# The beacon keys of sequences 2 to 7 loaded at the start and transposed early, with two projections moved

## The chip, the cores and the metric

The kernel runs on one core of a Trainium2 chip. The core has TensorE (PE in the profile; PEld is its weight load), VectorE (DVE), ScalarE (ACT), GpSimd (POOL) and SyncE (SP), and 16 DMA engines that move data between the device memory and the on-chip memories. SP, ACT and POOL can issue DMAs, each through a queue of its own (SPq, ACTq, POOLq in the profile). The metric is the device time of one execution in microseconds, lower is better.

## The reference

Attention with a few "beacon" keys in front, and then two matrix products with a leaky ReLU between them. Cut to what matters:

```python
# q, k, v: (8, 8, 576, 64); beacon_k, beacon_v: (8, 8, 16, 64)
k_all = np.concatenate([beacon_k, k], axis=2)         # 16 + 576 keys
v_all = np.concatenate([beacon_v, v], axis=2)
scores = np.matmul(q, k_all.transpose(0, 1, 3, 2)) / np.sqrt(64)
scores = np.where(causal, -1e9, scores)               # causal on the 576; beacon keys always seen
a = softmax(scores)
x = np.matmul(a, v_all)                               # -> (4608 tokens, 512)
h = x @ w_in                                          # w_in (512, 2048)
out = np.maximum(0.01 * h, h) @ w_out                 # w_out (2048, 512), out (4608, 512)
```

## The kernel before, in words

The work is cut into 32 pairs of heads: pair g is sequence g // 4 and two of its eight heads, whose 64 channels lie side by side in 128 partitions. For every pair the kernel needs queries and keys turned so that channels lie in partitions (qT, kT), the scores (keys in partitions, queries in columns), their exponentials in a buffer aT, the upper triangle set to zero on GpSimd (`triangle`, L281), and the values: aT against the values with a column of ones, so that the last column is the sum by which the rest is divided (`value`, L339; reciprocal L369 and product L370 on VectorE). The result is turned again into xT, either by transposes on PE (`x_transposes`) or by a DMA transpose on SP's queue (`x_turn`).

Behind that stand the two products, in nine chunks of 512 tokens. An up projection (`moe1`, L408: four matmuls of 128 x 512 at L413) makes 128 rows of the hidden layer, ScalarE applies the leaky ReLU (L420); 16 make a chunk. A down projection is a quarter of `moe2` (L446: four matmuls at L455); 16 make a chunk, and after every fourth VectorE copies the sum (L466) and SP stores it (L467). The first two down projections of a group of four read the first half of w_out, the other two the second half. In the code strings `u` is an up projection and `d` a down projection.

The beacon keys are 16 to a head. Those of all eight heads of a sequence fill 128 partitions; they are loaded (`load_beacon_k`, L176), cast to bf16 (`cast_beacon_k`, L179) and transposed on PE, two transposes to a sequence (`beacon_transposes`, L182). Sequences 0 and 1 are done at the very start and go straight into the first 16 columns of the key buffers. Sequences 2 to 7 go into bkT, from which GpSimd copies 16 columns per pair into a key buffer (`beacon_columns`, L219, step `b`), first for pairs 8 to 11.

The first eight pairs (sequences 0 and 1) follow an order written out by hand as strings of steps (L590 to L612), which `run` (L537) carries out. Each engine executes its own instructions in that order. The steps that matter here: `l` loads queries or keys of a pair with a cast, on POOL's queue; `q` and `k` turn them on PE (L235) with a copy on VectorE or ScalarE (L241); `s` is a quarter of a pair's scores with its exponential (L259, L268), `m` the triangles; `v` half of a pair's values; `V` a load of values (L206), `i` and `o` half of w_in and w_out (L123, L129), all on POOL's queue; `N` loads queries or keys of a later pair in their natural order (L163, POOL's queue) and `T` turns both of them by DMA transposes on SP's queue (L171); `y` is a turn of x by SP, `x` one by PE; `w` and `W` are matmuls of zeros whose result nobody reads (`unused`, L498, and `unused_ahead`, L510).

From pair 8 on the order is made by a list of events with due times (L638 to L677). The scores of pairs 8 to 31 are laid end to end and cut into tiles of 512 columns, three tiles to a `block` (L628); block m is due at 8.4 plus a step. Between events the loop puts in up and down projections by a linear plan (`fill`, L471).

The sums of PE live in two pools of PSUM: `ps_sc` for scores, and `ps_one`, four tiles shared by values, transposes, projections and the unused matmuls.

Of the kernel before, what the change touches and what calls it, by code (L numbers as in the profile page):

```python
# [8 lines left out]
FP32 = mybir.dt.float32  # L9
# [6 lines left out]
def kernel(  # L16
# [162 lines left out]
    def cast_beacon_k(b0, b1, copy):  # L179
        copy(out=bk[:, b0:b1], in_=bk_raw[:, b0:b1])  # L180
# [155 lines left out]

    xs, avs = {}, {}

    def value(g, half):  # L339
        b, hp = divmod(g, NPAIR)  # L340
        aT = probs[g]
        va = v_bufs[b % 2]
        if half == 0:
            xs[g] = (
                headpool.tile([128, 5, 2, D], BF16, name="x_nat", bufs=4),
                headpool.tile([128, 10], FP32, name="rec"),
            )
        x_nat, rec = xs[g]
        t0, t1 = ((0, 3), (3, 5))[half]
        av = avs.pop((g, half), None)  # L350
        if av is None:
            av = ps_one.tile([128, 512], FP32, name="av", tag="one")
        avv = av[:, 0 : (t1 - t0) * 132].rearrange("p (n w) -> p n w", w=66)
        for t in range(t0, t1):
            q0, _ = QT[t]
            for par in range(2):
                n = (t - t0) * 2 + par
                for c in range(t + 1):
                    a0 = acol(g, c, q0)
                    nc.tensor.matmul(  # L360
                        out=avv[:, n, 0 : D + 1],
                        lhsT=aT[0 : ROWS[c], par, a0 : a0 + 128],
                        rhs=va[0 : ROWS[c], c, 2 * hp + par, :],
                        start=(c == 0),
                        stop=(c == t),
                        skip_group_check=True,
                    )
        n0, n1 = t0 * 2, t1 * 2
        nc.vector.reciprocal(out=rec[:, n0:n1], in_=avv[:, :, D])  # L369
        nc.vector.tensor_tensor(  # L370
            out=x_nat[:, t0:t1].rearrange("p t e d -> p (t e) d"),
            in0=avv[:, :, 0:D],
            in1=rec[:, n0:n1, None].to_broadcast([128, n1 - n0, D]),
            op=ALU.mult,
        )
# [161 lines left out]
    def run(steps):  # L537
        for step in steps.split():
            op, a = step[0], [int(x) for x in step[1:].split(".")] if step[1:] else []
            if op == "s":  # L540
                score(*a)
            elif op == "m":
                mask(*a)
            elif op == "v":
                value(*a)
            elif op == "x":
                finish(*a)
            elif op == "l":
                load_qk(*a)
            elif op == "V":  # L550
                load_v_cast(*a)
            elif op == "N":
                load_natural(*a)
            elif op == "T":
                turn_pair(a[0])
            elif op == "y":
                x_turn(a[0])
            elif op == "q" or op == "k":
                t_q(a[0], 0 if op == "q" else 1, (dve, act)[a[1] if len(a) > 1 else 0])
            elif op == "b":  # L560
                beacon_columns(a[0], (dve, act, pool)[a[1]])
            elif op == "u":
                up()
            elif op == "P":
                moe1_early(*a)
            elif op == "d":
                down()
            elif op == "w":
                unused(*a)
            elif op == "W":  # L570
                unused_ahead(*a)
            elif op == "i":
                load_w_in(a[0])
            elif op == "o":
                load_w_out(a[0])
            else:
                raise ValueError(step)
# [11 lines left out]
    with order:  # L589
        load_first_keys()  # L590
        load_beacon_k(0, 2, nc.scalar)
        nc.vector.memset(blank, 0.0)  # L592
        run("l0.0 l1.0")
        make_identity(nc, ident)
        make_ones()
        run("l1.1 l2.0 l2.1 V0.0 V0.1 l3.0 l3.1 V0.2 V0.3 V0.4 l4.0 l4.1 i0")
        make_pads()
        unused(13, 256)
        cast_beacon_k(0, 2, nc.scalar.copy)
        beacon_transposes(0, 2)  # L600
        unused(13)
        nc.scalar.copy(out=k_nat0[:, :, 0], in_=first_k[:, 0])
        nc.vector.tensor_copy(out=k_nat0[:, :, 1], in_=first_k[:, 1])
        run("q0.1 k0 w2.384 s0.0 m0.0 w3.256 s0.1 q1 s0.2 m0.1 k1 s0.3 m0.2")
        run("w2.384 s1.0 m1.0 q2 s1.1 k2 w2.384 s1.2 m1.1 w2.384 s1.3 m1.2 W0.0.4 s2.0 m2.0 W0.0.4 s2.1 W0.0.2 q3 l5.0 l5.1 s2.2 k3 w3.384 v0.0 m2.1 s2.3 i1 m2.2 W0.1.4 s3.0 m3.0 v1.0 s3.1 v0.1 s3.2 v1.1 m3.1 l6.0 l6.1 s3.3 x0.1 m3.2")
        run("v2.0 V1.0 V1.1 q4 v2.1 x1 k4.1 v3.0 v3.1 x2.1 s4.0 s4.1 x3 m4.0 V1.2 V1.3 V1.4 l7.0 l7.1 u u s4.2 s4.3 q5 k5 m4.1 m4.2 u o0 u")
        load_beacon_k(2, B, nc.gpsimd)
        run("s5.0 s5.1 m5.0 u u u s5.2 s5.3 q6 k6 m5.1 m5.2 o1 u u s6.0 s6.1 m6.0 v4.0 u v4.1 y4 N8.0 N8.1 u u s6.2 s6.3 q7 k7 m6.1 m6.2 u")
        cast_beacon_k(2, B, nc.gpsimd.tensor_copy)
        run("u v5.0 u v5.1 N9.0 s7.0 s7.1 m7.0 d x5 v6.0 v6.1 T8 d s7.2 s7.3")  # L610
        beacon_transposes(2, B)
        run("m7.1 m7.2 N9.1 u b8.2 b9.2 b10.2 b11.2 x6 v7.0 T9 v7.1 d d N10.0 N10.1 d d V2.0 V2.1 x7 T10")  # L612


        FIRST = 2 * NPAIR
        COLS = FLAT[NKB]
        TILES = (NG - FIRST) * COLS // 512

        def tile_parts(n):
            at, end, parts = 512 * n, 512 * (n + 1), []  # L620
            while at < end:
                r, lo = divmod(at, COLS)
                hi = min(COLS, lo + end - at)
                parts.append((FIRST + r, lo, hi))
                at += hi - lo
            return parts

        def block(m):  # L628
            tiles = [tile_parts(n) for n in range(3 * m, min(3 * m + 3, TILES))]
            for n, parts in enumerate(tiles):  # L630
                stretch(parts, apart=n == 0)
            for parts in tiles:
                triangles(parts)

        def has_down():
            return done2[0] // NF < done1[0] // NF

        since = 0  # L638
        events = []
        for g in range(FIRST, NG):  # L640
            if g > FIRST + 2:
                events.append((g - 2.75, 0, run, ("N%d.0" % g,)))
                events.append((g - 2.45, 0, run, ("N%d.1" % g,)))
            if g > FIRST + 2:
                events.append((g - 1.75, 0, run, ("T%d" % g,)))
            if g > FIRST + 3:
                events.append((g - 1.65, 0, run, ("b%d.2" % g,)))
            at = g + (2.05 if g % NPAIR == NPAIR - 1 else 2.25)
            events.append((at, 3, value, (g, 0)))
            events.append((at + 0.37, 4, value, (g, 1)))  # L650
            events.append((at + 0.38, 5, x_turn, (g,)))
        for m in range((TILES + 2) // 3):
            events.append((FIRST + 0.4 + 1536 / COLS * m, 2, block, (m,)))
        ends = [FIRST]
        for g in range(FIRST, NG):
            events.append((g + 3.5, 2, finish, (g, 2)))
            if g % NPAIR == NPAIR - 1:
                ends.append(g + 3.5)
        for b in range(2, B):
            for n in range(2 if b == 2 else 0, NKB):  # L660
                events.append((4 * b + (-0.4 if b == 2 else -0.9) + 0.3 * n, 6, load_v_cast, (b, n)))
        events.sort(key=lambda e: e[:2])
        first_down[0] = 4
        w, d0 = 0, done1[0] + done2[0]
        for at, _, what, args in events:
            while w + 2 < len(ends) and at > ends[w + 1]:
                w, d0 = w + 1, done1[0] + done2[0]
            todo = 2 * NF * ready[0] - KEPT - d0
            aim = d0 + todo * (at - ends[w]) / (ends[w + 1] - ends[w])
            while done1[0] + done2[0] < aim and fill():  # L670
                pass
            if what is block:
                since = done1[0] + done2[0]
            elif what is value and not has_down():
                while done1[0] + done2[0] < since + 4 and fill():
                    pass
            what(*args)  # L677
        while done2[0] < NCH * NF:
            fill()
# [30 lines left out]
```

## Time and profile before

| | |
|---|---|
| median of five executions | 338.09 us |
| lowest and highest | 337.54 and 338.78 us |
| the profiled execution | 338.78 us |
| its span, first to last instruction | 337.1 us |
| PE matmul busy | 326.0 us |
| ScalarE busy | 187.1 us |
| GpSimd busy | 181.5 us |
| VectorE busy | 82.5 us |
| granted PE clock over the span | 1.000 |
| beacon keys of sequences 2 to 7: issue | 36.76 us, on POOL's queue |
| their cast on GpSimd | 47.67 us |
| their twelve transposes on PE | 50.32 us |
| first block of scores (pair 8) | 60.59 us |

A row of the timeline gives the start in us from the start of the span, the time from the first to the last of the merged instructions, engine, line, operation, what it writes and reads, how many, and in brackets the idle time of the engine just before it with what ended it. "issue" there means that the profile shows nothing it waited for. In the answer on DMA issues the last number is the time from the issue to the landing of the data. A row by stretches of time gives busy time of each engine in it, then the granted PE clock, the mean busy share of the DMA engines and GB/s. Matmul records are sometimes missing, so counts of 3 and 7 stand for 4 and 8.

### The profile page before, as it was taken

Reading aid. Unit: us, or ns where it says so; the run is one execution under the profiler, and the core shown is the slowest. Engines: PE = TensorE matmul, PEld = TensorE weight load, DVE = VectorE, ACT = ScalarE, POOL = GpSimd, SP = SyncE. Lnnn points to the kernel's source line nnn. Section 1 sums busy time; section 2 is a strip of 40 time slices with the busy share of each in tenths; the row PEclk is TensorE's granted clock in tenths of the full one; section 3 lists DMA queues with packets and bytes.
Section 4 is the critical chain, followed back from the end, with each engine's and each line's share of the span. In section 5 each row is a group of like instructions: output and inputs, shape, how many; then the busy total and the mean of one; then the engine's idle time right before and its main releaser. Section 6 shows DMA issues by size and latency. Waiting matters only on the chain.

```text
span 337.1 us, 7448 instructions
## 1 busy us (share of the span) xinstructions
PE 326.0 (97%) x2945; PEld 170.0 (50%) x2992; DVE 82.5 (24%) x201; ACT 187.1 (56%) x312; POOL 181.5 (54%) x355
## 2 busy tenths in 40 slices
PE   8999999899999999999999999999999999999996
PEld 5574465355554554554555555555455544444444
DVE  3472354021322113311321123212221310000111
ACT  5869762687565783488337843784378205633300
POOL 8895968878987785668656966674221000000000
PEclk9999999999999999999999999999999999999999
DMA  8999999999999999999999999999320120000012
GB/s 137 133 201 176 145 205 132 171 145 152 171 159 168 163 151 142 140 120 119 111 165 136 128 98 156 171 122 117 102 61 14 46 87 33 0 31 33 31 72 83
DMA packets 151922, 39.84 MB, mean 118 GB/s; under 512 B 143008, under 2 KB 145184, under 8 KB 151888
## 3 DMA queue, kind: packets, MB, share of 16 engines
q0 software_dynamic: 99824, 18.54, 85.9%
q1 hardware_dynamic: 51648, 20.64, 35.6%
q8 instruction: 23, 0.38, 0.5%
q10 hardware_dynamic: 416, 0.20, 0.2%
q14 instruction: 11, 0.09, 0.1%
HBM read 37.22 MB, written 9.44 MB: 138 GB/s over the span
## 4 chain that ended last, share of the span: by engine, by line
PE 82%; DMA 11%; POOL 3%; issue 2%; ACT 1%; DVE 0%; POOLq 0%; ACTq 0%; DVEq 0%
PE acc L455 35%; PE acc L413 33%; PE av L360 8%; PE sc L306 6%; DMA v_aug<-in_v_dram 5%; DMA w_in_sb<-in_moe_w_in_dram 4%; DMA k_nat<-in_k_dram 1%; DMA out_dram<-osb 1%; POOL v_aug L206 1%; POOL q_raw L151 0%; POOL aT L281 0%; PE sc L259 0%; POOL k_raw L151 0%; ACT aT L325 0%; POOL k_nat L163 0%
## 5 line engine op out<-in xcount | busy, mean ns | idle before, releaser
L413 PE MATMUL acc<-xT,w_in_sb 128*128 128x512 bf16 x553 | 134.4, 379 | 1.9 <-DVE osb L466 0.7
L455 PE MATMUL acc<-w_out_sb,gT 128*128 128x512 bf16 (+1 forms) x568 | 131.6, 373 | 1.5 <-issue 0.2
L420 ACT ACTIVATE gT<-acc 128x512 bf16<-128x512 f32 x144 | 83.5, 617 | 66.6 <-PE acc L413 64.9
L281 POOL TENSOR_SCALAR_AFFINE_SELECT aT<-aT 128x256 bf16<-128x256 bf16 (+2 forms) x160 | 57.7, 388 | 63.7 <-ACT aT L321 37.8
L455 PEld LDWEIGHTS <-gT 128*128 128x128 bf16 x592 | 55.3, 98 | 59.4 <-issue 0.7
L413 PEld LDWEIGHTS <-w_in_sb 128*128 128x128 bf16 x576 | 53.4, 98 | 62.7 <-issue 3.9
L321 ACT ACTIVATE aT<-sc 128x512 bf16<-128x512 f32 (+3 forms) x64 | 28.9, 520 | 57.2 <-PE sc L306 57.2
L325 ACT ACTIVATE aT<-sc 128x1024 bf16<-128x1024 f32 (+3 forms) x64 | 51.7, 890 | 0.0
L466 DVE COPY osb<-acc 128x512 f32<-128x512 f32 x35 | 24.2, 692 | 91.8 <-PE acc L455 84.1
L369 DVE RECIPROCAL rec<-av 128x6 f32<-128x6 f32 (+1 forms) x64 | 12.0, 188 | 132.6 <-PE av L360 132.6
L360 PEld LDWEIGHTS <-aT 128*128 128x128 bf16 (+1 forms) x960 | 36.5, 98 | 13.8 <-issue 3.3
L360 PE MATMUL av<-v_aug,aT 128*128 128x65 bf16 (+1 forms) x960 | 39.9, 194 | 1.4 <-DMA v_aug<-in_v_dram 1.3
L206 POOL DMA_DIRECT2D v_aug<-in_v_dram x40 | 34.0, 854 | 3.9 <-DMA w_in_sb<-in_moe_w_in_dram 3.6
L163 POOL DMA_DIRECT2D q_nat<-in_q_dram x48 | 34.8, 730 | 0.9
L163 POOL DMA_DIRECT2D k_nat<-in_k_dram x48 | 34.8, 728 | 0.5 <-issue 0.2
L370 DVE TENSOR_TENSOR x_nat<-av,rec 128x384 bf16<-128x384 f32 (+1 forms) x64 | 31.4, 491 | 2.2
L268 ACT ACTIVATE aT<-sc 128x1024 bf16<-128x1024 f32 (+3 forms) x32 | 26.0, 872 | 4.4 <-PE sc L259 2.7
L306 PE MATMUL sc<-qT,kT 64*128 64x80 bf16 (+22 forms) x384 | 21.8, 250 | 1.1 <-issue 1.1
L306 PEld LDWEIGHTS <-kT 64*128 64x128 bf16 x384 | 12.7, 94 | 14.7 <-issue 12.1
L259 PE MATMUL sc<-qT,kT 64*128 64x80 bf16 (+4 forms) x96 | 9.9, 284 | 0.1
L241 DVE COPY qT<-tp 128x576 bf16<-128x576 bf16 x7 | 5.3, 757 | 13.6 <-PE tp L235 13.6
L502 PE MATMUL av<-blank 128*128 128x256 bf16 (+2 forms) x40 | 7.0, 318 | 1.1 <-DVE blank L592 1.1
(45 smaller groups left out, 68.3 us busy)
## 6 DMA issues: line engine op xcount, KB each, us to landing
out_dram<-osb SPq DMA_DIRECT2D x35, 256.0 KB, 2.7
q_nat<-in_q_dram POOLq DMA_DIRECT2D x48, 72.0 KB, 4.7
k_nat<-in_k_dram POOLq DMA_DIRECT2D x48, 72.0 KB, 5.4
v_aug<-in_v_dram POOLq DMA_DIRECT2D x24, 128.0 KB, 6.6
w_in_sb<-in_moe_w_in_dram POOLq DMA_DIRECT2D x2, 1024.0 KB, 12.2
w_out_sb<-in_moe_w_out_dram POOLq DMA_DIRECT2D x2, 1024.0 KB, 12.2
q_raw<-in_q_dram POOLq DMA_DIRECT2D x8, 144.0 KB, 7.0
k_raw<-in_k_dram POOLq DMA_DIRECT2D x7, 144.0 KB, 7.5
```

The source lines that it names most:

```text
L163: nc.gpsimd.dma_start(out=t[:, :, par], in_=(q, k)[which][b, 2 * hp + par].rearrange("(t p) d -> p t d", p=NR),)
L206: nc.gpsimd.dma_start(out=dst[lo : ROWS[c], c, :, 0:D], in_=v[b, :, OFF[c] : OFF[c] + n].rearrange("h p d -> p h d"),)
L268: nc.scalar.activation(out=aT[:, :, c0 : c0 + w], in_=sc[:, :, 0:w], func=AF.Exp, scale=0.125)
L281: nc.gpsimd.affine_select(out=view, in_=view, compare_op=ALU.is_ge, fill=0.0, base=128 - n if lo == 0 else 0, channel_multiplier=-1, patte ...
L306: nc.tensor.matmul(out=(sc[par] if apart else sc[:, par])[:, at : at + b - a], lhsT=kT[ps_, c * 128 : (c + 1) * 128], rhs=qT[ps_, q0 : q0 ...
L321: nc.scalar.activation(out=probs[g][:, par, lo:hi], in_=sc[par][:, at : at + hi - lo], func=AF.Exp, scale=0.125)
L325: nc.scalar.activation(out=probs[g][:, :, lo:hi], in_=sc[:, :, at : at + hi - lo], func=AF.Exp, scale=0.125)
L360: nc.tensor.matmul(out=avv[:, n, 0 : D + 1], lhsT=aT[0 : ROWS[c], par, a0 : a0 + 128], rhs=va[0 : ROWS[c], c, 2 * hp + par, :], start=(c = ...
L370: nc.vector.tensor_tensor(out=x_nat[:, t0:t1].rearrange("p t e d -> p (t e) d"), in0=avv[:, :, 0:D], in1=rec[:, n0:n1, None].to_broadcast( ...
L413: nc.tensor.matmul(out=acc, lhsT=w_in_cols(fc, j), rhs=xT[:, j, i * 512 : (i + 1) * 512], start=(j == 0), stop=(j == NJ - 1),)
L420: nc.scalar.activation(out=gT[i][:, fc, :], in_=acc, func=AF.Prelu, alpha=0.01)
L455: nc.tensor.matmul(out=acc, lhsT=gT[i][:, fc, t * 128 : (t + 1) * 128], rhs=w_out_sb[:, fc, half * n : (half + 1) * n], start=(fc == 0), s ...
```

## The change

The beacon keys of sequences 2 to 7 are loaded by ScalarE's queue directly behind those of sequences 0 and 1, in place of POOL's queue between the two halves of w_out. Their cast goes from GpSimd to VectorE, ahead of the copies of pair 3, and their twelve transposes to the place just ahead of the first values, where they replace three unused matmuls of 384 columns (`w3.384`). One up projection goes from behind the values of pair 4 to ahead of them. The first block of the loop is due at 8.6 and not 8.4, which puts one up projection ahead of it and on POOL's queue one load of values and two of keys ahead of its triangles. A down projection is written ahead of the step N10; the two have no engine in common. A helper for beginning values early (`value_ahead`, step `e`) is added and not called by any step; with it the matmuls of `value` move into a function of their own.

```diff
+    begun = set()
+
+    def value_matmuls(g, half, avv, ts):
         b, hp = divmod(g, NPAIR)
         aT = probs[g]
         va = v_bufs[b % 2]
...
-        for t in range(t0, t1):
+        for t in ts:
             q0, _ = QT[t]
             for par in range(2):
-                n = (t - t0) * 2 + par
+                n = t % 3 * 2 + par
                 for c in range(t + 1):
...
+    def value_ahead(g):
+        if (g, 0) not in avs:
+            avs[g, 0] = ps_one.tile([128, 512], FP32, name="av", tag="one")
+        value_matmuls(g, 0, avs[g, 0][:, 0:396].rearrange("p (n w) -> p n w", w=66), (0, 1))
+        begun.add(g)
...
+        value_matmuls(g, half, avv, range(t0 + (2 if half == 0 and g in begun else 0), t1))
...
         load_beacon_k(0, 2, nc.scalar)
+        load_beacon_k(2, B, nc.scalar)
         nc.vector.memset(blank, 0.0)
...
-        run("w2.384 s1.0 m1.0 q2 s1.1 k2 w2.384 s1.2 m1.1 w2.384 s1.3 m1.2 W0.0.4 s2.0 m2.0 W0.0.4 s2.1 W0.0.2 q3 l5.0 l5.1 s2.2 k3 w3.384 v0.0 m2.1 s2.3 i1 m2.2 W0.1.4 s3.0 m3.0 v1.0 s3.1 v0.1 s3.2 v1.1 m3.1 l6.0 l6.1 s3.3 x0.1 m3.2")
+        run("w2.384 s1.0 m1.0 q2 s1.1 k2 w2.384 s1.2 m1.1 w2.384 s1.3 m1.2 W0.0.4 s2.0 m2.0 W0.0.4 s2.1 W0.0.2")
+        cast_beacon_k(2, B, nc.vector.tensor_copy)
+        run("q3 l5.0 l5.1 s2.2 k3")
+        beacon_transposes(2, B)
+        run("v0.0 m2.1 s2.3 i1 m2.2 W0.1.4 s3.0 m3.0 v1.0 s3.1 v0.1 s3.2 v1.1 m3.1 l6.0 l6.1 s3.3 x0.1 m3.2")
...
-        load_beacon_k(2, B, nc.gpsimd)
-        run("s5.0 s5.1 m5.0 u u u s5.2 s5.3 q6 k6 m5.1 m5.2 o1 u u s6.0 s6.1 m6.0 v4.0 u v4.1 y4 N8.0 N8.1 u u s6.2 s6.3 q7 k7 m6.1 m6.2 u")
-        cast_beacon_k(2, B, nc.gpsimd.tensor_copy)
+        run("s5.0 s5.1 m5.0 u u u s5.2 s5.3 q6 k6 m5.1 m5.2 o1 u u s6.0 s6.1 m6.0 u v4.0 u v4.1 y4 N8.0 N8.1 u s6.2 s6.3 q7 k7 m6.1 m6.2 u")
         run("u v5.0 u v5.1 N9.0 s7.0 s7.1 m7.0 d x5 v6.0 v6.1 T8 d s7.2 s7.3")
-        beacon_transposes(2, B)
-        run("m7.1 m7.2 N9.1 u b8.2 b9.2 b10.2 b11.2 x6 v7.0 T9 v7.1 d d N10.0 N10.1 d d V2.0 V2.1 x7 T10")
+        run("m7.1 m7.2 N9.1 u b8.2 b9.2 b10.2 b11.2 x6 v7.0 T9 v7.1 d d d N10.0 N10.1 d V2.0 V2.1 x7 T10")
...
-            events.append((FIRST + 0.4 + 1536 / COLS * m, 2, block, (m,)))
+            events.append((FIRST + (0.4 if m else 0.6) + 1536 / COLS * m, 2, block, (m,)))
```

More of the change, by code (lines that the diff above doesn't have):

```diff
@@ L337 @@
     xs, avs = {}, {}
-    def value(g, half):
+    begun = set()
+    def value_matmuls(g, half, avv, ts):
         b, hp = divmod(g, NPAIR)
@@ L342, in value @@
         va = v_bufs[b % 2]
+        for t in ts:
+            q0, _ = QT[t]
+            for par in range(2):
+                n = t % 3 * 2 + par
+                for c in range(t + 1):
+                    a0 = acol(g, c, q0)
+                    nc.tensor.matmul(
+                        out=avv[:, n, 0 : D + 1],
+                        lhsT=aT[0 : ROWS[c], par, a0 : a0 + 128],
+                        rhs=va[0 : ROWS[c], c, 2 * hp + par, :],
+                        start=(c == 0),
+                        stop=(c == t),
+                        skip_group_check=True,
+                    )
+    def value_ahead(g):
[3 more added lines that the diff above has]
+        begun.add(g)
+    def value(g, half):
         if half == 0:
@@ L353, in value @@
         avv = av[:, 0 : (t1 - t0) * 132].rearrange("p (n w) -> p n w", w=66)
-        for t in range(t0, t1):
-            q0, _ = QT[t]
-            for par in range(2):
-                n = (t - t0) * 2 + par
[L358 to L367, printed above, removed]
+        value_matmuls(g, half, avv, range(t0 + (2 if half == 0 and g in begun else 0), t1))
         n0, n1 = t0 * 2, t1 * 2
@@ L545, in run @@
                 value(*a)
+            elif op == "e":
+                value_ahead(*a)
             elif op == "x":
```

## The prediction

> **What bounds the kernel now.** I read the page first: busy time, then the slices.
>
> ```profile
> PE 326.0 (97%) x2945; PEld 170.0 (50%) x2992; DVE 82.5 (24%) x201; ACT 187.1 (56%) x312; POOL 181.5 (54%) x355
> ...
> DMA  8999999999999999999999999999320120000012
> ```
>
> TensorE (PE) is busy for 326.0 of 337.1 us, so the whole kernel has 11.1 us of PE idle time to give, plus PE work that serves nothing. The DMA row says that the transfer engines are full from the first slice on. A kernel whose PE is full can still be set by its loads in the beginning, so the next views are the timeline of PE, and beside it those of POOL and SP (the queues that issue the loads and the transposes), up to 62 us. PE's rows with a wait in them:
>
> ```profile
> 38.28 0.28 PE L360 MATMUL av<-v_aug,aT 128*128 128x65 bf16 x4 [0.67 <-DMA v_aug<-in_v_dram]
> ...
> 46.89 0.55 PEld L455 LDWEIGHTS <-gT 128*128 128x128 bf16 x4 [0.40 <-DMA w_out_sb<-in_moe_w_out_dram]
> ...
> 50.32 0.53 PE L186 MATMUL tp<-ident,bk 128*64 128x128 bf16 x12
> ...
> 60.59 0.85 PE L306 MATMUL sc<-qT,kT 64*128 64x512 bf16 x12 [1.07 <-issue]
> ```
>
> The reader should see three waits (0.67 for values, 0.40 for the first half of w_out, 1.07 ahead of the first block of scores) and the twelve beacon transposes at 50.32, which wait for nothing. POOL and SP in the same stretch:
>
> ```profile
> 36.76 0.85 POOL L177 DMA_DIRECT2D bk_raw<-in_beacon_k_dram x1
> ...
> 47.67 0.50 POOL L180 CAST bk<-bk_raw 128x384 bf16<-128x384 f32 x1 [2.95 <-DMA bk_raw<-in_beacon_k_dram]
> ```
>
> ```profile
> 54.28 1.22 SPq L171 DMA_TRANSPOSE qT<-q_nat  x1
> 55.60 1.22 SPq L171 DMA_TRANSPOSE kT<-k_nat  x1
> ```
>
> POOL stands 2.95 us for the beacon keys, which look like the thing to remove. Whether that matters is told by the issues with their time to landing, asked window by window:
>
> ```profile
> w_out_sb<-in_moe_w_out_dram POOLq DMA_DIRECT2D x1, 1024.0 KB, 10.7
> bk_raw<-in_beacon_k_dram POOLq DMA_DIRECT2D x1, 192.0 KB, 10.9
> w_out_sb<-in_moe_w_out_dram POOLq DMA_DIRECT2D x1, 1024.0 KB, 13.7
> ...
> kT<-k_nat SPq DMA_TRANSPOSE x1, 4.9
> ```
>
> Added to the issues at 35.98, 36.76, 39.30 and 55.60: w_out's first half lands at 46.7, the beacon keys at 47.6, w_out's second half at 53.0, and kT of pair 8 at 60.5. These are PE's own times: 46.89 for the first down projection, 53.05 for the third (the first to read the second half), 60.59 for block 0. The same holds at 25.76, where PE begins with w_in, issued at 13.26 and 12.4 us under way (25.7). So up to 60 us the landing times of one stream, POOL's loads in their order, pull PE along; it has 7 to 13 us of loads queued, and an earlier issue on POOL is worth nothing by itself. After 60.6 PE is full (7.9 of every 8 us) but for 0.69 us at 107.61, so a gain or loss held at block 0 should reach the end.
>
> **The change part by part.**
>
> 1. *Beacon load moved to the front of ScalarE's queue.* The 192 KB leave their place between the halves of w_out and go ahead of everything. Call the time that they cost the stream there d. All that lands up to w_out's first half is later by d; what is behind the old place is later by d less 0.9 (47.6 - 46.7, the stretch it took there). Bounds for d: not below 0, since work is only added ahead. 0 if they run wholly in the idle start (the engines' share is 0.03 from 1 to 2 us). 0.9 by the keys' own old stretch. 1.25 by the packets of the same queue: 0.2% of 16 x 337.1 us over 416 packets is 26 ns, times 768 rows of 256 bytes over 16 engines. 1.5 by the slowest value load: 1024 such rows between the landings at 36.2 and 38.2, so 2.0 x 0.75. It starts among the first loads, and from 2 to 3 us the engines' share is 0.83, so some 0.2 can be filled: I take 0.9 - 0.2 = 0.7, nearest to its own row. Ends 0 and 1.5.
>
> ```profile
> 1.00:2.00 1.00, 0.93 (x5) 0.68 (x6) 0.82 (x12) 1.00 (x1) 0.66 (x1) 1.00 0.03 7
> 2.00:3.00 1.00, 1.00 (x7) 0.67 (x6) 0.02 (x1) 0.18 (x2) 0.93 (x4) 1.00 0.83 194
> ```
>
> (The last two numbers are the DMA share and GB/s.) The issue itself, 0.44 on ScalarE's queue by the first beacon load, ends before that engine's table load (0.81 + 1.28). The path: w_in lands at 25.7 + 0.7, PE's first projection with it, and w_out's first half at 47.4: +0.7.
>
> The Trainium skill weighs this twice. "DMA: Bandwidth & Descriptors", section "Anatomy of one DMA", prices the moved bytes at bytes / 436e3: 0.45 us, an estimate, with which the sum below would be -1.07. The same page, "Queues, rings and completion order", has every engine take turns between the queues at packets, so that a second queue opens no second road; no row here shows 0.45 for such rows.
>
> 2. *POOL loses the issue (0.85), the wait (2.95) and the cast (0.50).* What is queued behind: w_out's second half and the natural loads of pair 8 are issued 0.85 earlier into a stream 7 to 13 us deep, 0. Pair 9's queries go some 3.6 earlier, 0, since SP issues pair 9's transposes only behind pair 8's, back to back from 54.28. Pair 9's keys stay behind the last masks of pair 7, which wait for ScalarE. So 0, with -0.1 as the other end (ScalarE's 50.37 exponential, which had waited for a mask).
>
> 3. *The cast on VectorE, ahead of pair 3's copies; two copies into bkT ahead of the first values.* The cast: by POOL's 0.50 and the 64x576 cast's 0.74, about 0.6, in an idle stretch of 2.75 us before 14.73. Cost 0 if the keys land by 14.1, 12.4 after their issue; the largest early load, first_k, took 4.0. The copies, 2 x 0.355, take 16.61 to 17.33; the first reciprocal moves from 16.83 to 17.33 and the one after it stays at 18.16, where it waits for PE. 0.
>
> 4. *Twelve transposes in place of three unused matmuls.* The old group ran from 15.74 to the next start at 16.24, 0.50; at 50.32 the transposes took 0.45 to the next start. 0. They leave their old place, where PE was full: -0.45, other end -0.2, because the values of pair 7 then come that much closer to their masks (the last ended at 52.5, PE needs it some 0.9 after the first of those values, now 51.45).
>
> Here a rule speaks against: "TensorE: Matmul & The Clock Gate", section "PE-mode transpose", says that transposes do not count as work for the clock. The trace: granted clock 1.00 in every window from 4 to 26 us, though 18 transposes at a time stand between short matmuls; and a true fall shows as pace, 13 matmuls of 256 columns in 2.95 us at the start against three in 0.50 at 6.89. By the rule a half clock as long as that start would add some 2.4, of which 0.65 (a wait for values at 19.56) and 0.67 (next item) are slack: +1.1, sum +0.3. I go by the row.
>
> 5. *One up projection before pair 4's values.* It covers the 0.67 wait. But PE then comes to 46.47 + 0.7 - 0.67 and w_out is there at 47.4: what was saved is waited out. 0, other end -0.67.
>
> 6. *One up projection (4 x 0.216 = 0.86) before block 0.* PE was through at 59.52, now 59.52 + 0.7 - 0.45 = 59.77, and 60.63 with the projection; kT of pair 8 lands at 60.5 + 0.7 - 0.9 = 60.3. The wait is gone: -1.07, other end -0.2 if the landing does not move back by 0.9. On POOL, block 0's masks now stand behind one value load (0.90) and two key loads (1.45): they end at 62.0 + 2.35 + 1.56 = 65.9 instead of 64.8, and block 1's exponentials on the same tile began at 66.39; 0, margin some 0.4. The third down projection moved ahead of N10 changes no engine's own order; 0. The helper for values begun early is called by no step; 0.
>
> Sum: +0.7 - 0.45 - 1.07 = -0.82. In the profiled execution 338.78 (span 337.1 and 1.7 around it) becomes 337.96; that one was the slowest of five, 0.69 over their median of 338.09, so the forecast is 337.3. Ends: d of 0 with the other parts gives -1.5, of 1.5 gives 0.0.
>
> **Rivals.** (a) The load hides wholly, and w_out is early enough for part 5 too: -1.5 to -2.2, 336.2 on average. For it: nothing moves before 2 us. Against: share 1.06 from 3 us on. (b) Nothing gained: d is 0.9 to 1.6, and front and back cancel; 338.0 (-0.6 to +0.1). For it: the 1.25 and the 1.5. (c) Slower: rows of 256 bytes among first_k and the first queries hold the whole stream more than their own time. Place 2 to 9 us, price one to one through w_in and w_out; slower from d = 1.52, by over 0.2% from d = 2.2; at 2.5, 339.1. For it: from 12 to 14 us, with small rows, the engines' share is 3.36 in 2 us at only 128 GB/s, and w_out took 5.9 us behind the last keys with transposes of another queue beside it, w_in 4.6. Against: the first beacon load of that queue took 2.0 us in all.
>
> **How the numbers follow.** Forecast 0.42, (a) 0.10, (b) 0.28, (c) 0.20. 0.2% is 0.68 us, about what a measurement of this kernel can tell from no change. Faster by that: (a) and most of the forecast, 0.46; within: (b) and the rest, 0.33; slower: (c) and a little of (b), 0.21. Some 0.3 more on either side is for the wait at 107.61, which can go or double when PE is early there. Range 336.3 to 338.8; the forecast's own 336.8 to 337.7.
>
> **What would show it.** Right: the first w_in matmul at 26.4, the first down projection at 47.5 behind a wait of about 1 us for w_out, no L186 group at 50, block 0 with no wait before it and a projection ahead. Wrong: w_in at 25.8 (d is 0, rival a) or after 27.3 (c); block 0 still waiting, so that the transposes did not come earlier; VectorE's cast waiting beyond 14.1, or matmuls from 16 us at half their pace.

## The result, and the profile after

The changed kernel is faster by 0.38%: the ratio of its time to that of the kernel before is 0.9962, interval [0.9946, 0.9977]. On the 338.56 us median of the kernel before (86 executions) that is -1.3 us, between -0.8 and -1.8; -0.82 was forecast. The ratio compares undisturbed executions alone, so it is not that of the medians (337.95 us for all 44 executions of the changed kernel): 16 of the 44, and 4 of the 86, lie at 343 to 345 us, and the mean over all executions is 339.9 us for the changed kernel and 339.0 us for the one before.

The profiled execution took 335.95 us, with a span of 334.2 us against 337.1. A second one of each gave 334.7 and 337.7. So single profiles show a gain of 2.9 to 3.0 us, more than twice the 1.3: the profiled executions of the changed kernel (335.95 and 336.43 us) lie below its median, those of the kernel before (338.78 and 339.43 us) above its own. Profiles tell here where time went, and not how much.

The page of the changed kernel, busy time and the row of the transfer engines:

```profile
PE 325.6 (97%) x2942; PEld 169.9 (51%) x2989; DVE 82.8 (25%) x202; ACT 186.6 (56%) x312; POOL 180.3 (54%) x353
...
DMA  8999999999999999999999999999310120000012
```

PE's busy time is 0.4 us less than before (326.0 then), so nearly all of what the profile gains is idle time. The timeline of PE in the changed kernel has the places that the prediction named (start, length, engine and line, what is written and read, and in brackets a wait before it):

```profile
6.27 0.47 PE L235 MATMUL tp<-ident,q_raw 64*64 64x64 bf16 x18 [0.74 <-DMA q_raw<-in_q_dram]
...
15.98 0.53 PE L186 MATMUL tp<-ident,bk 128*64 128x128 bf16 x12
...
25.18 0.38 PE L424 MATMUL acc<-xT,w_in_sb 128*128 128x512 bf16 x1
...
37.54 0.53 PE L351 MATMUL av<-v_aug,aT 128*128 128x65 bf16 x12
...
45.53 1.04 PE L466 MATMUL acc<-w_out_sb,gT 128*128 128x512 bf16 x4
...
50.94 0.71 PE L351 MATMUL av<-v_aug,aT 128*128 128x65 bf16 x18 [0.25 <-ACT gT L431]
...
57.80 1.03 PE L424 MATMUL acc<-xT,w_in_sb 128*128 128x512 bf16 x4
58.76 0.61 PE L306 MATMUL sc<-qT,kT 64*128 64x512 bf16 x6
```

The first queries and the first projection with w_in in the kernel before:

```profile
5.36 0.47 PE L235 MATMUL tp<-ident,q_raw 64*64 64x64 bf16 x18 [0.28 <-DMA q_raw<-in_q_dram]
...
25.76 1.90 PE L413 MATMUL acc<-xT,w_in_sb 128*128 128x512 bf16 x7
```

One wait is longer: 0.74 us and not 0.28 for the first queries, which land 0.9 later than before. Every other wait for a load is gone: 0.16, 0.36 and 0.65 between 14 and 20 us, 0.67 at 38, 0.40 at 46.9, 1.07 ahead of block 0. The first projection with w_in starts at 25.18 (25.76 before), the first down projection at 45.53 (46.90), block 0 at 58.76 (60.59), and it has one up projection (57.80) ahead of it that it had not. The issues of the changed kernel, with size and time to landing:

```profile
bk_raw<-in_beacon_k_dram ACTq DMA_DIRECT2D x1, 192.0 KB, 5.0
...
w_in_sb<-in_moe_w_in_dram POOLq DMA_DIRECT2D x1, 1024.0 KB, 12.2
w_out_sb<-in_moe_w_out_dram POOLq DMA_DIRECT2D x1, 1024.0 KB, 9.6
w_out_sb<-in_moe_w_out_dram POOLq DMA_DIRECT2D x1, 1024.0 KB, 12.6
...
kT<-k_nat SPq DMA_TRANSPOSE x1, 5.4
```

Added to the issues at 12.04, 34.51, 36.99 and 52.64: w_in's first half lands at 24.2 (25.7 before), w_out's halves at 44.1 and 49.6 (46.7 and 53.0), kT of pair 8 at 58.0 (60.5). So 192 KB were put ahead of POOL's stream, and what comes behind them lands *earlier*, by 1.5 us at w_in and by 2.6 at w_out. The stream picks up between 9 and 18 us: by the packets' records POOL's queue has moved 0.86 MB by 9 us in both kernels, and by 18 us 2.05 MB in the kernel before and 2.29 MB in the changed one. Windows of the kernel before, and then of the changed one (the last two numbers are the DMA share in us and GB/s, over all queues):

```profile
12.00:14.00 2.00, 2.00 (x20) 0.91 (x18) 0.00 (x0) 2.00 (x3) 0.87 (x2) 1.00 3.36 128
14.00:18.00 4.00, 3.48 (x79) 2.42 (x77) 2.27 (x4) 2.83 (x5) 4.00 (x13) 1.00 2.14 141
```

```profile
12.00:14.00 2.00, 2.00 (x24) 0.82 (x18) 1.16 (x3) 2.00 (x4) 2.00 (x5) 1.00 2.49 151
14.00:18.00 4.00, 4.00 (x92) 2.70 (x91) 2.52 (x6) 3.55 (x6) 4.00 (x12) 1.00 1.51 167
```

More bytes move, and the DMA share is lower (2.49 against 3.36 in 2 us). This share adds up the times that packets are under way and divides by 16, so it can pass the length of the window; a lower one for more bytes says that each byte is under way for less time. VectorE, where the cast and the copies now are, pays nothing that reaches PE:

```profile
12.80 0.35 DVE L180 CAST bk<-bk_raw 128x384 bf16<-128x384 f32 x1
...
16.76 0.71 DVE L195 COPY bkT<-tp 64x384 bf16<-64x384 bf16 x2
17.51 0.20 DVE L380 RECIPROCAL rec<-av 128x6 f32<-128x6 f32 x1
```

### The profile page after: what moved, and what is told of

The parts are those of the page before. It is cut to its first block, busy times and chain, and to the rows that moved or that the text cites. A ratio compares the mean times of both kernels' runs of the same rounds, so it can differ in the third digit from the quotient of the medians.

```text
span 334.2 us, 7441 instructions
## 1 busy us (share of the span) xinstructions
PE 325.6 (97%) x2942; PEld 169.9 (51%) x2989; DVE 82.8 (25%) x202; ACT 186.6 (56%) x312; POOL 180.3 (54%) x353
## 4 chain that ended last, share of the span: by engine, by line
PE 94%; DMA 2%; issue 1%; ACT 1%; DVE 0%; DVEq 0%; ACTq 0%; POOLq 0%
PE acc L424 37%; PE acc L466 37%; PE av L351 9%; PE sc L306 6%; PE sc L259 2%; PE tp L235 1%; DMA q_raw<-in_q_dram 1%; DMA out_dram<-osb 1%; ACT aT L268 1%; PE tp L393 1%; PE av L513 1%; PE av L525 0%; DVE osb L477 0%; ACT gT L431 0%; PE tp L186 0%
## 5 line engine op out<-in xcount | busy, mean ns | idle before, releaser
L477 DVE COPY osb<-acc 128x512 f32<-128x512 f32 x35 | 24.2, 692 | 90.8 <-PE acc L466 78.2
```

## The experiments

The theory after this result: the early load on a second queue speeds up the stream (POOL's loads in their order), and nearly all of the gain is that. The rivals: the gain comes from the moved transposes and projections, as the prediction had it; or from taking the load out of POOL's work; or one lucky execution. The kernels e1 to e8 ran on one chip, e9 to e12 on another, each beside runs of the kernel before on the same chip.

**Both kernels once more.** No edit.

> The kernel before, once more, for its profile. Theory A (the early beacon load itself makes POOL's stream of loads land earlier): this run looks like the first profile of before, the first half of w_in lands at 25.7 +- 0.4 and PE begins with it at 25.8, the first half of w_out lands at 46.7 +- 0.6, block 0 waits 1 us. Theory B (the stream's speed differs by 1 to 2 us from execution to execution, and the two profiles were one slow and one fast draw): w_in lands anywhere from 24 to 26, and w_out's first half with it.

Kernel before: 339.43 us, w_in's first half landed at 25.2, w_out's at 46.3. Its PE waited for values 1.15, 0.28 and 0.51 near 38 to 41 us and 0.74 at block 0.

> The changed kernel, once more. Theory A: w_in's first half lands at 24.3 +- 0.4, PE begins with it at 25.2 and block 0 starts at 58.8 +- 0.4 without a wait. Theory B: w_in lands anywhere from 24 to 27, and the span follows it. Time: 1.0 to 1.6 us under the kernel before.

Changed kernel: 0.9965 [0.9932, 0.9998]. Landings 23.7 and 43.2, first w_in matmul 25.18, first down projection 45.58, block 0 at 58.82. The earlier landings came in both profiles.

**The beacon part alone.** The early load, VectorE's cast and the early transposes; the projections stay where they were.

```diff
+        load_beacon_k(2, B, nc.scalar)
...
+        cast_beacon_k(2, B, nc.vector.tensor_copy)
+        run("q3 l5.0 l5.1 s2.2 k3")
+        beacon_transposes(2, B)
...
-        load_beacon_k(2, B, nc.gpsimd)
...
-        cast_beacon_k(2, B, nc.gpsimd.tensor_copy)
...
-        beacon_transposes(2, B)
```

> Only the beacon keys are moved (load, cast, transposes); both projections stay where they were. Theory A: the loads come early, so neither projection is needed to cover a wait: no wait for values at 37, none for w_out, block 0 at 58.2 with a wait of at most 0.3; time within 0.3 us of the whole change, about 1.2 under the kernel before. My forecast's sum: +0.7 for the load, -0.45 for the transposes, and half of block 0's wait, -0.5: only 0.3 under the kernel before.

0.9961 [0.9928, 0.9994], as much as the whole change; landings 23.6 and 43.7. PE in its timeline:

```profile
25.21 0.81 PE L413 MATMUL acc<-xT,w_in_sb 128*128 128x512 bf16 x3
...
45.60 1.04 PE L455 MATMUL acc<-w_out_sb,gT 128*128 128x512 bf16 x4
...
58.51 0.85 PE L306 MATMUL sc<-qT,kT 64*128 64x512 bf16 x12 [0.48 <-issue]
```

With no projection moved, no wait for values at 38 is left, and 0.48 of the 1.07 at block 0 (at most 0.3 was expected): kT of pair 8 lands at 58.4 and not 60.5.

**The projections alone.** The beacon part as before.

```diff
-... s6.0 s6.1 m6.0 v4.0 u v4.1 y4 N8.0 N8.1 u u s6.2 ...
+... s6.0 s6.1 m6.0 u v4.0 u v4.1 y4 N8.0 N8.1 u s6.2 ...
...
-            events.append((FIRST + 0.4 + 1536 / COLS * m, 2, block, (m,)))
+            events.append((FIRST + (0.4 if m else 0.6) + 1536 / COLS * m, 2, block, (m,)))
```

> Only the two projections are moved; the beacon keys stay as before. My forecast's sum: the one ahead of pair 4's values gives nothing (PE waits 1.1 instead of 0.4 for w_out), the one ahead of block 0 takes its wait, 0.86 of 1.07: 0.9 us under the kernel before. Theory B, and theory A as well if the loads are as in the first profile of before: the same 0.9. If the time is that of the kernel before within 0.3, the projections do nothing and all of the gain is the beacon keys'.

1.0001 [0.9966, 1.0035]. No gain was measured; one of 0.9 us (0.9973) would still be inside the interval. Its PE, and then its two loads (issued at 13.07 and 35.52):

```profile
46.38 0.82 PE L455 MATMUL acc<-w_out_sb,gT 128*128 128x512 bf16 x3
...
59.00 1.03 PE L413 MATMUL acc<-xT,w_in_sb 128*128 128x512 bf16 x4
60.53 0.85 PE L306 MATMUL sc<-qT,kT 64*128 64x512 bf16 x12 [0.51 <-PE acc L413]
```

```profile
w_in_sb<-in_moe_w_in_dram POOLq DMA_DIRECT2D x1, 1024.0 KB, 12.4
w_out_sb<-in_moe_w_out_dram POOLq DMA_DIRECT2D x1, 1024.0 KB, 10.8
```

Landings 25.4 and 46.3, as before. The profile does what the prediction said: the values near 38 no longer wait, PE waits 0.59 instead of 0.40 for w_out at 46.38, and block 0 starts where it did, with one projection more already done.

**The early load alone, as pure extra work.** The kernel before, with the same 192 KB loaded at the start into a tile that nothing reads. The late load, POOL's cast and the late transposes all stay.

```diff
+    bk_spare = singles.tile([128, B - 2, D], FP32, name="bk_spare")
...
+        nc.scalar.dma_start(out=bk_spare, in_=beacon_k[2:B].rearrange("b h n d -> (h n) b d"))
```

> The kernel before with the early load added to it, into a tile that nobody reads; the late load, cast and transposes stay. It measures the early load by itself. Theory A1 (a second queue that is busy from 2 to 6 us makes POOL's stream faster, whatever the rest): the first queries land at 6.2, w_in's first half at 24.0 +- 0.4, w_out's first half at 43.9 +- 0.6, the late beacon keys 0.9 behind it; block 0 still 0.5 late for the late transposes; time 0.7 to 1.0 us under the kernel before. Theory A2 (the stream is faster because something else of the change is gone or moved): w_in lands at 25.4 + 0.9 or later, and the time is 0.5 to 1 us above the kernel before, as my forecast's part 1 had it.

0.9967 [0.9934, 1.0000]. PE, and the two loads (issued at 12.03 and 33.74):

```profile
25.12 1.95 PE L414 MATMUL acc<-xT,w_in_sb 128*128 128x512 bf16 x7
...
45.46 1.04 PE L456 MATMUL acc<-w_out_sb,gT 128*128 128x512 bf16 x4
...
48.88 0.53 PE L187 MATMUL tp<-ident,bk 128*64 128x128 bf16 x12
...
58.51 0.85 PE L307 MATMUL sc<-qT,kT 64*128 64x512 bf16 x12 [0.42 <-issue]
```

```profile
w_in_sb<-in_moe_w_in_dram POOLq DMA_DIRECT2D x1, 1024.0 KB, 11.7
w_out_sb<-in_moe_w_out_dram POOLq DMA_DIRECT2D x1, 1024.0 KB, 9.2
```

Landings 23.7 and 42.9. A kernel that only does *more* than the one before has the early landings of the changed kernel, with the twelve transposes still in their late place, at 48.88. This is the strongest run for the theory, though its own interval just reaches 1.

**The same bytes on the same queue in wide rows.** 128 rows of 1536 bytes of w_in, unread, in place of 768 rows of 256.

```diff
+    bk_spare = singles.tile([128, (B - 2) * D], FP32, name="bk_spare")
...
+        nc.scalar.dma_start(out=bk_spare, in_=moe_w_in[0:128, 0 : (B - 2) * D])
```

> The kernel before with an added early load of the same 192 KB on the same queue, but as 128 rows of 1536 bytes of w_in in place of 768 rows of 256 bytes, into a tile that nobody reads. If it is the small rows that do it (they keep that queue busy until 6.3): w_in's first half lands as in the kernel before, 25.4 or up to 0.5 later. If any traffic in a second queue does: 24.0 +- 0.4 and a time 0.7 to 1.0 us under the kernel before.

1.0087 [1.0050, 1.0123], slower. w_in landed early here too (24.3), but the first queries came at 6.67 and PE ran slow after them. PE's timeline, and then windows (the number behind POOL's count is the granted clock):

```profile
6.72 0.47 PE L236 MATMUL tp<-ident,q_raw 64*64 64x64 bf16 x18 [1.25 <-DMA q_raw<-in_q_dram]
...
29.09 1.09 PE L414 MATMUL acc<-xT,w_in_sb 128*128 128x512 bf16 x3
```

```profile
8.00:10.00 2.00, 2.00 (x25) 0.91 (x25) 0.41 (x1) 1.43 (x2) 2.00 (x3) 0.58 1.92 166
10.00:12.00 2.00, 2.00 (x36) 0.98 (x30) 1.47 (x2) 1.76 (x3) 1.67 (x4) 0.50 1.80 153
...
20.00:22.00 2.00, 2.00 (x37) 1.28 (x31) 1.67 (x4) 1.29 (x3) 2.00 (x5) 1.00 1.12 210
```

At half clock until some 18.6 us (by the 0.86 of the window from 18 to 20), PE comes to w_in 3.9 us later than in the changed kernel, and the early landing is worth nothing. It was not this execution alone: the granted clock is 0.985 or lower in six of the eight executions compared. What rows of 256 bytes do for the rest of the stream can't be read from this run, since PE, and with it all later issues, is late.

**The beacon part, its load first on POOL's queue.** As the beacon part alone, but issued by GpSimd.

```diff
-        load_beacon_k(2, B, nc.scalar)
+        load_beacon_k(2, B, nc.gpsimd)
```

> As the beacon-only kernel, but the early load is issued by POOL, as its first, ahead of the first queries: same bytes, same place in time, no second queue. If the second queue is what speeds the stream: w_in's first half lands at 25.4 + 0.9 or later and the time is within 0.5 us of the kernel before or above it. If only the early position of the bytes counts: as with ScalarE's queue, 24.0, and 1.2 us under the kernel before.

1.0058 [1.0020, 1.0097], slower. PE, and the loads (issued at 15.02 and 36.74):

```profile
6.86 0.47 PE L235 MATMUL tp<-ident,q_raw 64*64 64x64 bf16 x18 [0.80 <-DMA q_raw<-in_q_dram]
...
27.23 0.38 PE L413 MATMUL acc<-xT,w_in_sb 128*128 128x512 bf16 x1
```

```profile
w_in_sb<-in_moe_w_in_dram POOLq DMA_DIRECT2D x1, 1024.0 KB, 11.2
w_out_sb<-in_moe_w_out_dram POOLq DMA_DIRECT2D x1, 1024.0 KB, 10.5
```

Landings 26.2 and 47.2: 0.5 to 1.0 later than before at w_in and 0.5 to 0.9 at w_out, which is what the prediction's +0.7 had in mind. So neither the early place nor the freed late one makes the gain by itself: against e3 only the queue differs, and with it POOL's first load of queries, issued at 2.32 and not at 1.33. The ratio stands for 2.0 us, more than the landings explain; in three of the eight executions compared the granted clock was 0.984 or 0.985 (1.00 in the profile), so part of the loss can be PE's clock.

**POOL's first issues later.** A rival by which the early load only holds POOL's first loads back, and their spacing does the rest: a memset on GpSimd ahead of its first issue.

```diff
+    idle = singles.tile([128, 1024], BF16, name="idle")
...
+        nc.gpsimd.memset(idle, 0.0)
```

> The kernel before with about 1 us of clearing an unused tile on POOL ahead of its first load; no load is added. It tells whether a later start of POOL's loads is what makes them run faster afterwards (in the changed kernel the first queries land 0.9 later and all from the third load on land earlier). If so: first queries at 6.3, w_in's first half at 24.5 or earlier. If not: all loads land 0.5 to 1.2 later than in the kernel before, w_in at 26.2, time 0.3 to 1.0 us above.

0.9994 [0.9968, 1.0020]. The delay came out at only 0.36 us, so this tests little. Its landings, 25.0 and 44.8, are earlier than in the kernel before and e4, though it has no early load. One execution each doesn't tell whether that is the delay or scatter.

**The early load 2 us later.** The changed kernel, with the load issued behind ScalarE's first cast, at 2.85 us.

```diff
-        load_beacon_k(2, B, nc.scalar)
...
+        load_beacon_k(2, B, nc.scalar)
```

> The changed kernel with its early load issued some 2 us later, behind ScalarE's cast of the first beacon keys (about 3.2 us in place of 1.3). Theory A1a (small rows in a second queue anywhere in the first 8 us keep POOL's stream fast): the first queries land at 5.3 again, w_in's first half at 24.2 or earlier, block 0 at 58.8 or earlier; time 0 to 0.5 us under the changed kernel, 1.2 to 1.7 under the kernel before. Theory A1b (what counts is that the second queue is full while POOL's first loads start, from 3 to 6 us): w_in at 25.2 or later, w_out's first half at 46 or later, and the time is that of the kernel before within 0.5.

0.9997 [0.9961, 1.0032]. The first queries are on time (5.20), the landings 24.3 and 44.8, and the profiled span is 334.5 us: its profile looks like a gain, its time shows none, though the interval does not exclude the changed kernel's 0.9962 either.

**Twice and half the early load, unread.** 384 KB in two loads, and 96 KB, added to the kernel before.

```diff
+    bk_spare = singles.tile([128, 12, D], FP32, name="bk_spare")
...
+        nc.scalar.dma_start(out=bk_spare[:, 0:6], in_=beacon_k[2:8].rearrange("b h n d -> (h n) b d"))
+        nc.scalar.dma_start(out=bk_spare[:, 6:12], in_=beacon_k[2:8].rearrange("b h n d -> (h n) b d"))
```

> The kernel before with two early loads of the 192 KB into a tile that nobody reads. If more traffic there helps more: w_in's first half under 23.5. If the first half of the effect is all there is and the added bytes cost their own time: w_in at 23.7 + 0.9 = 24.6 and the first queries at 7.2, time between that with one early load (0.33% under the kernel before) and the kernel before.

1.0003 [0.9971, 1.0035]. The first queries landed at 6.64, PE waited 1.49 us for them, and the granted clock over the profiled execution was 0.975; its landings (25.3 and 47.0) can't be set beside those of the others.

```diff
+    bk_spare = singles.tile([128, 3, D], FP32, name="bk_spare")
...
+        nc.scalar.dma_start(out=bk_spare[:, 0:3], in_=beacon_k[2:5].rearrange("b h n d -> (h n) b d"))
```

> The kernel before with an early load of half the size (three sequences, 96 KB), into a tile that nobody reads. If the effect goes with the time that the second queue is busy: first queries at 5.8, w_in's first half at 24.4 to 24.8, time half-way, 0.5 us under the kernel before. If it is all or nothing: either as with 192 KB (w_in at 23.7) or as without (25.4).

1.0000 [0.9971, 1.0029]; landings 24.5 and 44.7, between the two groups, first queries 5.80. Neither size brought a time that could be told from no change. The changed kernel itself was not run beside these on their chip, so a difference between the chips is not excluded as a reason.

**No late load at all.** The late load and POOL's cast are left out and the tile is zeroed by VectorE, so the beacon columns of sequences 2 to 7 are left out of the computation.

```diff
+        nc.vector.memset(bk[:, 2:B], 0.0)
...
-        load_beacon_k(2, B, nc.gpsimd)
...
-        cast_beacon_k(2, B, nc.gpsimd.tensor_copy)
```

> The kernel before without any load of the beacon keys of sequences 2 to 7 and without POOL's cast; VectorE sets their cast tile to zero in its idle start, and the late transposes stay. So the beacon columns of sequences 2 to 7 are left out of the computation. It measures what POOL's issue, wait and cast are worth by themselves. My forecast's part 2 said 0 for PE: w_in at 25.4, w_out's first half at 46.5, its second half 0.9 earlier than in the kernel before (52.0), kT of pair 8 with it (59.6), so block 0 starts 0.5 to 0.9 earlier; time 0.5 to 0.9 us under the kernel before, if the front is all that counts, and the same within 0.5 us otherwise.

0.9997 [0.9972, 1.0023]. In its profile w_out's second half landed 5.8 us behind the first and not 6.3, but taking the issue, the 2.95 us wait and the cast off POOL, and the 192 KB off its queue, brought no time that can be told from no change.

Taken together, in the profiles: the four with the 192 KB of beacon keys issued on ScalarE's queue at 1.3 us (the changed kernel twice, e3, e5) have w_in landing at 23.6 to 24.3 and w_out at 42.9 to 44.1. The three with none and nothing else altered up to there (the kernel before twice, e4) have 25.2 to 25.7 and 46.3 to 46.7. The medians lie 1.7 and 2.9 us apart; e8, with no early load, lies between the groups. In time, the four ratios of the first group are 0.9961 to 0.9967, and the three kernels without an early load (e4, e8, e12) are at 0.9994 to 1.0001. The intervals of e2 and e3 only just leave out 1, that of e5 reaches it, and that of e4 overlaps them; the 44 executions of the changed kernel carry the verdict that it is faster. That the early load is the cause rests on the landings and on these ratios together. Against it stand e9, e10 and e11 on the other chip, where an early load brought no measured time.

Why the second queue speeds the first one up stays open. In the packets' records of the first profiles, POOL's queue had 13 packets that took over 0.3 us each between 3 and 9 us in the kernel before (6.9 us in all) and none in the changed one; e1 and e4 had 15 and 18, e7 52, and e2, e3 and e5 no more than 2. By 20 us POOL's queue had moved 2.45 MB before and 2.71 MB after. So the long packets go with the slow stream, but e9 has 19 of them with landings of 24.3 and 44.8, and e8 has 27 with 25.0 and 44.8; with one profile each, that is a correlation and no cause.

## Why the prediction was right, and where not

The direction was right and the size near: -0.82 forecast, -1.3 measured, inside the range. That the sum came near is luck: its first term had the wrong sign, and the two gains that it was added to, -0.45 and -1.07, were not measured on their own. By the prediction's own signs the mechanism was wrong: no first w_in matmul at 26.4, no wait of about 1 us for w_out.

- *Part 1, the step that failed.* The early load was to cost the stream d = +0.7, with the bound "not below 0, since work is only added ahead". Measured, d is about -1.7 at w_in and -2.9 at w_out, with the pure extra load too. The bound took the stream as a line in which an added piece can only push the rest. The load's own cost was sized well: its packets took 1.2 us of each engine's time (1.5 us for all packets of ScalarE's queue in the first 9 us, 0.3 before), near the 1.25 of the bound. What failed is that this cost pushes the rest back one to one; the rest got faster by more. The 0.2 that "can be filled" was no room either: the share of 0.83 adds up packets under way and passes 1 per us later on. The prediction's rows had a sign against the bound: a share of 3.36 in 2 us for 128 GB/s from 12 to 14 us is a stream with many packets under way and few bytes moved, which leaves room to get faster. Put on POOL's own queue, the same load did cost 0.5 to 1.0 at w_in: there the reasoning held. The signal set for "wrong" (w_in at 25.8) came, and went beyond: w_in was there at 24.2, and PE, which had no other wait left, came to it by its own work at 25.18.
- *Rival (a)* was nearest in its end, w_out early and no wait left, but its reason (hidden in the idle start) is not what happened: the load is not hidden, since the first queries come 0.9 later and PE starts on them 0.9 later, and the gain comes after it. Rival (b) says 338.0 for changes of -0.6 to +0.1; the middle of these would be 337.8.
- *The second queue.* The Trainium skill, "DMA: Bandwidth & Descriptors", section "Issuing engines are not separate DMA queues", says that issuing from several engines saves only the time to initiate a transfer. The measurement differs: the same load issued by ScalarE (e3) and by POOL (e7) gave 0.9961 and 1.0058, 3.3 us apart, and w_in at 23.6 and 26.2, where the issue on POOL took 0.97.
- *Part 2* (POOL's issue, wait and cast go) at 0: e12 agrees within 0.3%. A wait of 2.95 us on that engine was worth nothing that could be measured, which fits a queue that was 7 to 13 us deep.
- *Part 3* at 0: the keys landed at 6.3, the cast ran at 12.80 in 0.35 us (0.6 was estimated), the first reciprocal started at 17.51 (17.33 was forecast), and PE waited for none of them.
- *Part 4* at -0.45: not to be told. e5 keeps the late transposes and is at 0.9967, e3 moves them and is at 0.9961; 0.45 us is 0.13%. At 15.98 they cost PE what the unused matmuls had: 0.45 to the next start, 0.50 before. The granted clock stayed at 1.00 there, as the row had it; no run has transposes for long enough to test the clock rule itself.
- *Part 5* at 0: the reason given (PE would then wait for w_out) holds for the old landing: in e4 w_out lands at 46.3 and PE waits 0.59 for it. With the early stream both waits are gone with no projection moved (e3).
- *Part 6* at -1.07: the mechanism was seen (a projection at 57.80, no wait at block 0), but most of the wait goes by kT's earlier landing alone (0.48 left in e3), and e4, which has this part with the old stream, gave no measured time. Of the gap from w_out's first to its second half 0.9 was to go; 6.3 became 5.5.
- *Where a gain ends.* Block 0 starts 1.8 us earlier with 0.86 of a projection ahead of it, together 2.7, and the span is 2.9 shorter: held to the end within the profiles. How much of this is scatter between executions, only many executions tell: they give 1.3.

## What to carry to other kernels

Here a transfer added ahead of a busy stream, on another queue, made the stream faster, in a kernel whose windows showed a large DMA share for few bytes. For such a term put a bound on both sides of zero, and try the transfer as extra work that nothing reads, which separates the stream from every other part of a change. Check what the transfer delays first: in e6 the first loads that PE waits for came late, and the early stream was worth nothing. Take sizes from many executions: two profiles of each kernel agreed on 2.9 to 3.0 us where the times show 1.3.

## What the runs showed of the hardware that was not expected

- With 192 KB in rows of 256 bytes issued on ScalarE's queue at 1.3 us, POOL's queue landed its loads 1.7 us (w_in) to 2.9 us (w_out) earlier, by medians of four and three profiles; with the same load at the head of POOL's queue (one profile) they landed later. Why is open, and on the other chip no early load brought a measured time.
- A wait of PE for its first queries, after the matmuls that serve no result, was followed by a fallen clock when it was long. With 0.74 us (changed kernel) and 0.80 us (e7) the granted clock stayed at 1.00; with 1.25 us (e6) it was 0.58 from 8 to 10 us and 0.50 from 10 to 12, and back at 1.00 only from 20. The Trainium skill, "TensorE: Matmul & The Clock Gate", section "HAM oscillation — how this bites in real kernels", puts the harmful gap above about 3.4 us; here 1.25 went with a fall. The record of all executions goes the same way: of the kernels whose profile has the first queries landing at 6.2 us or later (the changed kernel, e3, e5, e6, e7, e10), 27 of 110 executions have a mean granted clock of 0.985 or less, 10 of them among the 57 of the changed kernel; of the others (the kernel before on the two chips, e4, e8, e9, e11, e12), none of 152 has less than 0.990. So an early load that delays the first queries risks the clock. That the wait is the cause is argued, since no run changed the wait alone.
